# The first layer of a mixture of experts by seven block products on 512 tokens

## The chip, the cores and the metric

The program runs on one core of one Trainium2 chip. The metric is the device time of one execution in microseconds (us), lower is better. The core's engines are PE (TensorE, matrix products), DVE (VectorE), ACT (ScalarE), POOL (GpSimd) and SP (SyncE, which here only issues DMAs). Each works through its own list of instructions in order and waits on semaphores for the others.

## The reference

Attention over q, k, v (2 batches, 8 heads, 576 positions, width 64) gives x of 1152 tokens by 512. Then come two mixtures of experts:

```
p = domain_probs / (domain_probs.sum(-1, keepdims=True) + 1e-09)      # first mixture, 4 experts, all used
for e in range(4):
    h = np.maximum(x @ w1[e], 0.0)                                    # 512 -> 1024
    out += p[:, e:e + 1] * (h @ w2[e])                                # 1024 -> 512
logits = out @ w_gate + modality_bias[modality_id]                    # second mixture, 8 experts
e_idx = argmax(logits)                                                # each token uses one expert
```

The change is in the first mixture, in `x @ w1[e]`.

## The kernel before

Three parts follow one another. The attention and the first steps of the first mixture are ordered by a planner with costs and due times (`Plan`, written out by `emit`). The rest of the first mixture is written by hand as a list of steps. A planned end does the gate and the second mixture.

**Precision.** A float32 product is made of three passes of a rounded format: a tensor is split into a high and a low part (`xhi`, `xlo`; `w1h`, `w1l`; `hh`, `hl`), and high by high, high by low and low by high are added up in PSUM. To split a weight tile, ACT makes the high part (`w_hi`) and DVE the low part (`w_lo`), each over 128x1024 numbers.

**Steps.** The tokens are cut in chunks 0 to 3 of 256, 256, 256 and 384 tokens. `SEG` lists runs of (expert, chunks). A step is (s, c, f): entry s of `SEG`, chunk c, and one of 8 blocks f of 128 hidden units. `mm1` (L693 by the profile) makes `x @ w1` for it in 12 matmuls of 256 columns (4 slices of the width by 3 passes). ACT makes `hh` by a ReLU (L699) and DVE makes `hl` (L704). `mm2` (L712 to L714) multiplies by `w2` in 3 matmuls of 512 columns for each 128 tokens and adds up over f. At f = 7 DVE adds p times the result to `y` (L722, `y_add`). The code writes `mm1` of a step and then `mm2` of the step before, so that PE has work while `hh` and `hl` are made. A scheduler of the compiler then orders each engine's list by what is ready when. Weights come in as 512-KB loads (`raw`, SP) and are split one or two steps ahead.

**Gate work between the steps.** `gate_consts` (called at step (2, 1, 1) before) loads the gate's weights four times in a form spread over all partitions (`st`, L834). POOL copies six of eight experts' columns of each into `wgT` (L835), and later the other two into `wgU` (L859). It also makes a small table `wg` on DVE (L828) and turns the tokens' modality ids into `mf` (DVE, L841), which PE transposes (L843, `ps<-ident,mf`) and DVE combines into `bias`. `dot` (L871, on DVE) multiplies a 128x512 block of finished `y` by one expert's whole row of `wgT` or `wgU` and sums; so the first `dot` needs all four copies. `FIRST` says at which entry of `SEG` a chunk is first summed.

**Memory.** The tiles `st` and the small gate tiles live in the pools `m2raw` and `gate`, which are opened after the attention's pools are closed and take over their memory.

Of the kernel before, what the change touches and what calls it, by code (L numbers as in the profile page):

```python
# [8 lines left out]
F32 = mybir.dt.float32  # L9
F32R = mybir.dt.float32r  # L10
# [7 lines left out]
D = 64  # L18
# [69 lines left out]
TARGET = 3600  # L88
HARD = 3400
TRC = 1  # L90
RUNS = 0
TRR = .75
DP = (50, 20, 0)
DQ = (0, 0, 0, 0, 0, 0)
DMC = 1.23
# [195 lines left out]
def moe_chain_kernel(ctx, tc, q, k, v, probs, w1, w2, mod, wg, mbias, v1, v2, out):  # L291
# [17 lines left out]
    def bank():  # L309
        return ps.tile([128, 512], F32, tag="ps", name="ps")  # L310
# [90 lines left out]
    def tr(nm, n, f):  # L401
        T["pt", nm, n, f] = pt = bank()
        pv = pt[:, 0:RR * RP].rearrange("c (p r) -> c r p", r=RR)
        for r in range(RR):
            x = T[nm, n][:, f]
            if n < RUNS:
                nc.tensor.transpose(pv[0:64, r, :], x[:, D * r:D * r + D], ident[:RP, :RP])
                nc.tensor.matmul(pv[64:128, r, :], x[:, D * (RR + r):D * (RR + r) + D], ident[:RP, :RP], start=True, stop=True)
            else:
                nc.tensor.transpose(pv[:, r, :], x[:, 128 * r:128 * r + 128], ident[:RP, :RP])  # L410
# [245 lines left out]
    W = {}  # L656
    NU = 4

    def w_load(kind, s, j):
        t = rawp.tile([128, KD, 256] if kind == 1 else [128, 2, DM], F32, tag="raw", name="raw")  # L660
        e = SEG[s][0]
        if kind == 1:
# [24 lines left out]
    ACC = {}  # L687

    def mm1_part(o, s, c, f, kk):
        hi, lo = W[1, s, f // 2]  # L690
        fs = slice(128 * (f % 2), 128 * (f % 2) + 128)
# [14 lines left out]
    def mm2_part(s, c, f, t):  # L706
        if f == 0:
            ACC.setdefault((s, c), {})[t] = bank()
        hi, lo = W[2, s, f // 2]
        hh, hl = HT[s, c, f]  # L710
        ts, a = slice(128 * t, 128 * t + 128), ACC[s, c][t]
        nc.tensor.matmul(a, hh[:, ts], hi[:, f % 2, :], start=(f == 0), stop=False)  # L712
        nc.tensor.matmul(a, hh[:, ts], lo[:, f % 2, :], start=False, stop=False)  # L713
        nc.tensor.matmul(a, hl[:, ts], hi[:, f % 2, :], start=False, stop=(f == NF - 1))  # L714
# [834 lines left out]
    if True:  # L1549
# [22 lines left out]
        P.slow, P.lag, P.also = 1.0, 0.0, {}  # L1572
        runs = [(g, c) for g, (_, cs) in enumerate(SEG) for c in cs]
        steps = [z + (f,) for z in runs[:runs.index(QFROM)] for f in range(NF)]
        KP = len([x for x in steps if x[0] < NPSEG]) + 1
        for g in range(NPSEG + 1):
            for j in range(NU):
                for kind in (1, 2):
                    p_w(kind, g, j, (WPR + WST * j if g == 0 else WPG + .1 * (NU * g + j)) + .5 * (kind - 1), WLO)
        for i, z in enumerate(steps[:KP]):  # L1580
            p_mm1(*z, MPR + 1.2 * i)
            if i:
                p_mm2(*steps[i - 1], MPR + 1.2 * i + .5)
        def fillers():
# [11 lines left out]
        m2p["raw"] = ctx.enter_context(tc.tile_pool(name="m2raw", bufs=1, side="right", reuse_waits="tile"))
        m2p["g"] = ctx.enter_context(tc.tile_pool(name="gate", bufs=2, side="right", reuse_waits="tile"))
        y1 = m2p["g"].tile([128, 5, DM], F32, tag="y1", name="y1", bufs=1)
        yacc.extend(y1[:, t, :] for t in range(5))
        dots = [(i, x) for i in range(4) for x in range(V)]  # L1600
        for s, c, f in steps[KP:]:
            mm1(s, c, f)
            mm2(*prev)
            prev = (s, c, f)
            r = runs.index((s, c))
            if c == SEG[s][1][0] and s > NPSEG and f < 2:
# [60 lines left out]
```

## Time and profile before

| | us |
|---|---|
| three runs, median | 625.64 (624.74 to 628.19) |
| the profiled execution | 624.6 |
| its span in the trace | 622.7 |
| PE busy in it | 600.4 (96%) |
| DVE / ACT / POOL busy | 381.8 / 255.2 / 86.9 |
| mean granted PE clock | 0.992 of full |

The span is the time from the first to the last instruction; 1.9 us of the execution lie around it. Busy shares are means over stages. Matmul records overlap (each is shown for longer than the distance to the next), so the pace is read from starts.

### The profile page before, as it was taken

The page shows a single profiled execution, that of the slowest core. Times are in us where ns is not written, and L with a number is a line of the kernel's source. Part 1 is how long each engine was busy: PE and PEld are TensorE (multiplying, and loading weights), DVE is VectorE, ACT ScalarE, POOL GpSimd, SP SyncE. Part 2 cuts the span into 40 slices and gives each one's busy share as a digit, 9 for nine tenths or more (in the row PEclk, how much of TensorE's full clock was granted, in tenths as well). Part 3 has the DMA queues.
Part 4 walks back from the last instruction along what each step waited for, and adds up shares of the span by engine and source line. Part 5 has one row for each costly group of instructions (what it writes and reads, how often), then busy time and mean ns, then how long its engine had stood idle before and what let it go on. Part 6 is the DMA issues. An engine that isn't in the chain of part 4 may idle for free. (4 is left out here: it accounts for less than half of the span.)

```text
span 622.7 us, 11280 instructions
## 1 busy us (share of the span) xinstructions
PE 600.4 (96%) x4265; PEld 527.5 (85%) x4270; DVE 381.8 (61%) x817; ACT 255.2 (41%) x595; POOL 86.9 (14%) x120
## 2 busy tenths in 40 slices
PE   7689999999999999999999999999999999999994
PEld 4578888889798999999989989999988898888983
DVE  4898678767525618564342455439955789669781
ACT  5855256542313411113321334313343555559581
POOL 3333113115000001000000000001130035201011
PEclk9999999999999999999999999999999999999997
DMA  7999944107511510001330345605295404867830
GB/s 148 156 219 221 234 135 136 36 2 213 168 35 61 177 34 2 1 1 52 119 101 1 102 135 173 200 5 132 42 352 193 143 15 131 286 194 254 293 136 20
DMA packets 84465, 78.67 MB, mean 126 GB/s; under 512 B 36135, under 2 KB 67248, under 8 KB 84402
## 3 DMA queue, kind: packets, MB, share of 16 engines
q1 hardware_dynamic: 82482, 73.13, 42.0%
q0 software_dynamic: 1920, 4.73, 2.2%
q8 instruction: 35, 0.57, 0.4%
q14 instruction: 28, 0.23, 0.1%
HBM read 77.49 MB, written 5.07 MB: 133 GB/s over the span
## 5 line engine op out<-in xcount | busy, mean ns | idle before, releaser
L693 PE MATMUL ps<-xhi,w1h 128*128 128x256 f32 (+1 forms) x512 | 153.8, 300 | 0.0
L693 PE MATMUL ps<-xhi,w1l 128*128 128x256 f32 (+1 forms) x512 | 151.8, 297 | 0.0
L693 PE MATMUL ps<-xlo,w1h 128*128 128x256 f32 (+1 forms) x512 | 151.6, 296 | 0.2 <-DVE xlo L609 0.2
L699 ACT ACTIVATE hh<-ps 128x256 fp32r<-128x256 f32 (+1 forms) x128 | 52.4, 410 | 209.6 <-PE ps L693 201.2
L704 DVE SCALAR_TENSOR_TENSOR hl<-ps,hh 128x256 fp32r<-128x256 f32 (+1 forms) x128 | 57.9, 454 | 121.2 <-ACT hh L699 121.0
L712 PE MATMUL ps<-w2h,hh 128*128 128x512 f32 x288 | 115.7, 402 | 0.0
L714 PE MATMUL ps<-w2h,hl 128*128 128x512 f32 x288 | 113.6, 395 | 1.2 <-DVE hl L704 1.2
L713 PE MATMUL ps<-w2l,hh 128*128 128x512 f32 x288 | 113.3, 393 | 0.0
L693 PEld LDWEIGHTS ps<-xhi,w1h 128*128 128x128 f32 x512 | 96.5, 188 | 5.9 <-issue 0.6
L693 PEld LDWEIGHTS ps<-xlo,w1h 128*128 128x128 f32 x512 | 96.4, 188 | 5.3 <-DVE xlo L609 0.4
L693 PEld LDWEIGHTS ps<-xhi,w1l 128*128 128x128 f32 x512 | 96.4, 188 | 0.0
L714 PEld LDWEIGHTS ps<-w2h,hl 128*128 128x128 f32 x288 | 54.0, 188 | 14.8 <-DVE hl L704 2.3
L712 PEld LDWEIGHTS ps<-w2h,hh 128*128 128x128 f32 x288 | 54.2, 188 | 8.0 <-issue 0.4
L713 PEld LDWEIGHTS ps<-w2l,hh 128*128 128x128 f32 x288 | 54.2, 188 | 6.9
L673 DVE TENSOR_TENSOR w2l<-raw,w2h 128x1024 fp32r<-128x1024 f32 x32 | 39.4, 1230 | 29.3 <-ACT w2h L414 29.2
L414 ACT ACTIVATE w1h<-raw 128x1024 fp32r<-128x1024 f32 x47 | 49.7, 1057 | 17.6 <-PE ps L693 14.9
L673 DVE TENSOR_TENSOR w1l<-raw,w1h 128x1024 fp32r<-128x1024 f32 x32 | 39.1, 1221 | 10.8 <-ACT w1h L414 10.1
L414 ACT ACTIVATE w2h<-raw 128x1024 fp32r<-128x1024 f32 x28 | 29.7, 1061 | 37.6 <-PE ps L714 35.6
L1222 DVE TENSOR_TENSOR w2l<-r,w2h 128x1024 fp32r<-128x1024 f32 x28 | 33.9, 1221 | 14.5 <-ACT w2h L414 14.5
L985 POOL DMA_INDIRECT tab<-tg,si x9 | 9.6, 1062 | 209.8 <-DVE tg L982 188.3
L414 ACT ACTIVATE w2h<-r 128x1024 fp32r<-128x1024 f32 x28 | 29.4, 1058 | 17.0 <-PE ps L1345 9.2
L1321 PE MATMUL ps<-xh,w1h 128*128 128x256 f32 x128 | 36.0, 281 | 0.0
(287 smaller groups left out, 933.1 us busy)
## 6 DMA issues: line engine op xcount, KB each, us to landing
raw<-in_moe_w_dram SPq DMA_DIRECT2D x85, 512.0 KB
r<-in_moe_w_dram SPq DMA_DIRECT2D x35, 512.0 KB
v<-in_v_dram SPq DMA_DIRECT2D x32, 80.0 KB
kraw<-in_k_dram SPq DMA_DIRECT2D x16, 147.0 KB
qraw<-in_q_dram SPq DMA_DIRECT2D x16, 147.0 KB
vq<-in_v_dram SPq DMA_DIRECT2D x8, 288.0 KB
ys<-y SPq DMA_DIRECT2D x9, 256.0 KB
st<-in_moe_w_gate_dram SPq DMA_DIRECT2D x4, 512.0 KB
```

The source lines that it names most:

```text
L414: e.activation(out=out, in_=in_, func=ACTF.Copy, scale=scale)
L673: e.tensor_tensor(out=l, in0=W.pop(("raw", kind, s, j)), in1=h.bitcast(F32), op=ALU.subtract)
L693: nc.tensor.matmul(o, wt[:, kk, fs], xt[:, kk, :], start=(kk == 0 and m == 0), stop=(kk == KD - 1 and m == 2))
L699: nc.scalar.activation(out=hh, in_=o, func=ACTF.Relu)
L704: nc.vector.scalar_tensor_tensor(out=hl, in0=o, scalar=0.0, in1=hh.bitcast(F32), op0=ALU.max, op1=ALU.subtract)
L712: nc.tensor.matmul(a, hh[:, ts], hi[:, f % 2, :], start=(f == 0), stop=False)
L713: nc.tensor.matmul(a, hh[:, ts], lo[:, f % 2, :], start=False, stop=False)
L714: nc.tensor.matmul(a, hl[:, ts], hi[:, f % 2, :], start=False, stop=(f == NF - 1))
L985: i = nc.gpsimd.indirect_dma_start(out=tab, out_offset=bass.IndirectOffsetOnAxis(ap=Z["si"][:, t:t + 1], axis=0), in_=G["tg"][:, 3 * c + t ...
L1222: e.tensor_tensor(out=l, in0=R["raw", u], in1=h.bitcast(F32), op=ALU.subtract)
L1321: nc.tensor.matmul(pt, wt[:, kk, fs], xt[:, kk, :], start=(i == 0), stop=(i == 3 * KD - 1))
```

## The change

**What it does.** Entry 3 of `SEG`, expert 3 on all four chunks, becomes two entries, expert 3 on chunks 0 and 1 and expert 3 on chunks 2 and 3; its weights are loaded and split twice. Then `PAIR = (2, 3)`: experts 2 and 3 on the tokens 0 to 511 (chunks 0 and 1 side by side). For expert 2 the hidden blocks (0, 4) and (1, 5) are still done by ordinary steps. The other two pairs of expert 2 and all four of expert 3 are six units. A unit takes two hidden blocks and both chunks, splits the width in halves, and computes the 2x2 product of blocks by Strassen's seven products: `s_mm1` has 7 products of 2 slices by 3 passes, 42 matmuls of 256 columns, where four steps have 48. `s_mm2` has the same 24 matmuls of 512 columns as four `mm2`.

**What feeds a unit.** `s_xf` and `s_xc` make five sums and differences of blocks of x once, split in high and low. `s_w` makes for each unit five sums of weight blocks (`sa`, `sb`) and splits seven blocks. `w_load` brings the w1 columns of a pair as two DMAs of 128 columns. Within a unit the products M4 and M3 go to one bank, `r34`, and ACT copies it (`s34`); M1 goes to a second bank, `r16`, and ACT copies that half (`uv`); M2 and M5 are then added on top of `r34` and M6 and M7 on `r16`. DVE forms the four combinations. The order of the code is `s_mm1` of a unit, then `s_mm2` of the unit before. The expert's second layer is as before.

**What moves.** `gate_consts` is now called at step (4, 2, 1), the second step after the units, `gate_cols` at (4, 2, 4), and the `dot`s start after it. The pools `m2raw` and `gate` are opened only after the pool `seven` of the units is closed, and take over its memory.

```diff
-SEG = ((0, (0, 1)), (1, (0, 1)), (2, (0, 1)), (3, (0, 1, 2, 3)), (2, (2, 3)), (1, (2,)), (0, (2, 3)), (1, (3,)))
+SEG = ((0, (0, 1)), (1, (0, 1)), (2, (0, 1)), (3, (0, 1)), (3, (2, 3)), (2, (2, 3)), (1, (2,)), (0, (2, 3)), (1, (3,)))
+PAIR = (2, 3)
-FIRST = {0: 0, 1: 0, 2: 3, 3: 3}
+FIRST = {0: 0, 1: 0, 2: 4, 3: 4}
...
+    def unit(s, f):
+        return (f % NU, f // NU) if s in PAIR else (f // 2, f % 2)
...
+        if s in PAIR:
+            if kind == 1:
+                for h in range(2):
+                    nc.sync.dma_start(out=t[:, :, 128 * h:128 * h + 128],
+                                      in_=w1[e, :, FF // 2 * h + 128 * j:FF // 2 * h + 128 * j + 128].rearrange("(k p) f -> p k f", p=128))
...
+    def s_w(s, j):
...
+        tt(out=a[:, 0:2].rearrange("p s (k f) -> p (s k) f", k=2), in0=raw[:, :, 1], in1=raw[:, :, 0], op=ALU.subtract)
...
+        nc.scalar.activation(out=ah, in_=a, func=ACTF.Copy)
...
+        tt(out=al, in0=a, in1=ah.bitcast(F32), op=ALU.subtract)
...
+    def s_mm1(s, j):
...
+        def prod(o, i, start):
+            h, l, n, (xh, xl) = m[i]
+            for k in range(2):
+                f = slice(128 * k, 128 * k + 128)
+                for q, (w, x) in enumerate(((h, xh), (h, xl), (l, xh))):
+                    nc.tensor.matmul(o, w[:, n, f], x[:, k], start=start and k == 0 and q == 0, stop=k == 1 and q == 2, skip_group_check=not start)
...
+        r34, r16 = bank(), bank()
+        A, B = slice(0, 256), slice(256, 512)
+        prod(r34[:, B], 4, True)
+        prod(r34[:, A], 3, False)
+        s34, uv, c = t("s34"), t("uv"), t("sc")
+        nc.scalar.activation(out=s34, in_=r34, func=ACTF.Copy)
+        prod(r16[:, A], 1, True)
+        nc.scalar.activation(out=uv[:, B], in_=r16[:, A], func=ACTF.Copy)
+        nc.vector.tensor_tensor(out=uv[:, A], in0=s34[:, A], in1=s34[:, B], op=ALU.add)
+        nc.vector.tensor_tensor(out=uv[:, B], in0=uv[:, A], in1=uv[:, B], op=ALU.add)
+        prod(r16[:, B], 6, False)
+        prod(r34[:, B], 2, False)
+        prod(r34[:, A], 5, False)
+        (h1, l1), (h2, l2) = SH[s, j] = [[t(f"s{x}{i}", F32R) for x in "hl"] for i in range(2)]
+        nc.scalar.activation(out=h2, in_=r34, func=ACTF.Relu)
+        nc.vector.scalar_tensor_tensor(out=l2, in0=r34, scalar=0.0, in1=h2.bitcast(F32), op0=ALU.max, op1=ALU.subtract)
+        prod(r16[:, A], 7, False)
...
+        units = [(2, 2), (2, 3)] + [(3, j) for j in range(NU)]
...
+        for i, (x, j) in enumerate(units):
+            s_mm1(x, j)
+            if i == 0:
+                mm2(*prev)
+            else:
+                s_mm2(*units[i - 1])
...
+            if prev[0] in PAIR:
+                s_mm2(*units[-1])
+                ctxs.close()
+                m2p["raw"] = ctx.enter_context(tc.tile_pool(name="m2raw", bufs=1, side="right", reuse_waits="tile"))
+                m2p["g"] = ctx.enter_context(tc.tile_pool(name="gate", bufs=2, side="right", reuse_waits="tile"))
...
-            if (s, c, f) == (NPSEG, 1, 1):
+            if (s, c, f) == (FIRST[2], 2, 1):
                 gate_consts()
-            if (s, c, f) == (FIRST[2], 2, 1):
+            if (s, c, f) == (FIRST[2], 2, 4):
                 gate_cols()
-            if s >= FIRST[2] and c >= 2 and (s, c, f) > (FIRST[2], 2, 1) and dots:
+            if (s, c, f) > (FIRST[2], 2, 4) and dots:
                 dot(*dots.pop(0))
```

**PE around the transposition of `mf`.** Before, it stands between two steps of expert 3 and waits for nothing; L714 is the third pass of `mm2`, L693 is `mm1`.

```order
L714 MATMUL ps<-w2h,hl 128x512 [waits DVE_49]
L712 MATMUL ps<-w2h,hh 128x512
L713 MATMUL ps<-w2l,hh 128x512
L714 MATMUL ps<-w2h,hl 128x512
L843 MATMUL ps<-ident,mf 128x9
L693 MATMUL ps<-xhi_92,w1h 128x256
L693 MATMUL ps<-xlo_96,w1h 128x256
```

After, the same instruction (L954) stands behind `mm2` of (4, 2, 1), in front of the next `mm1` (L695).

```order
L721 MATMUL ps<-w2h,hl 128x512 [waits DVE_49]
L719 MATMUL ps<-w2h,hh 128x512
L720 MATMUL ps<-w2l,hh 128x512
L721 MATMUL ps<-w2h,hl 128x512
L954 MATMUL ps<-ident,mf 128x9 [waits DVE_49]
L695 MATMUL ps<-xhi_93,w1h 128x256
L695 MATMUL ps<-xlo_97,w1h 128x256
```

It now carries a wait for DVE, and two steps of expert 3 on chunk 2 lie between it and the end of the units.

**DVE around the cast of `mf`.** Before (L841), it stands among splits of weights (L673) and `hl`.

```order
L828 CAST wg<-wr 128x4x8 [waits DMAHW4_49,DMAHW0_49]
L829 TENSOR_TENSOR wg<-wr,wg 128x4x8 [waits DVE_49]
L673 TENSOR_TENSOR w2l<-raw,w2h 128x1024 [waits DMAHW2_49,Activation_49]
L704 SCALAR_TENSOR_TENSOR hl<-ps,hh 128x256 [waits Activation_49]
L673 TENSOR_TENSOR w1l<-raw,w1h 128x1024 [waits DMAHW3_49,PE_49,Activation_49]
L841 CAST mf<-mi 9x128 [waits DMAHW3_49]
```

After (L952), it stands behind three `dot`s (L982), the first of which waits for POOL; five more `dot`s and five small operations lie between it and the next `hl` (L706).

```order
L706 SCALAR_TENSOR_TENSOR hl<-ps,hh 128x256 [waits Activation_49]
L939 CAST wg<-wr 128x4x8 [waits DMAHW7_49]
L940 TENSOR_TENSOR wg<-wr,wg 128x4x8 [waits DVE_49]
L982 SCALAR_TENSOR_TENSOR junk,l<-y_99,wgT 128x512 [waits Pool_49]
L982 SCALAR_TENSOR_TENSOR junk,l<-y_99,wgT 128x512 [waits DVE_49] x2
L952 CAST mf<-mi 9x128 [waits DMAHW3_49]
L982 SCALAR_TENSOR_TENSOR junk,l<-y_99,wgT 128x512 [waits DVE_49]
L957 COPY m<-ps 128x9 [waits PE_49]
```

**SP and the loads of `st` after the change.** Three of the four (L945) carry a wait for PE; POOL copies `wgT` and `wgU` of the first, then of the second, and so on.

```order
L945 DMA st_3459<-in_moe_w_gate_dram 128x1024 [waits PE_49]
L935 DMA tab<-ti 128x164 [waits Pool_49]
L945 DMA st_3462<-in_moe_w_gate_dram 128x1024 [waits PE_49]
L945 DMA st_3465<-in_moe_w_gate_dram 128x1024 [waits PE_49]
L937 DMA wr<-in_moe_w_gate_dram 128x4x8 [waits DMAHW4_49]
L945 DMA st_3468<-in_moe_w_gate_dram 128x1024 [waits DMAHW0_49]
```

They stood at step (2, 1, 1) before, and now stand where the last unit's tiles come free.

**ACT at the end of the planned part.** Before, a `w2h` that waits for PE stands ahead of two `hh` (L699) in a row.

```order
L699 ACTIVATE hh<-ps 128x256 [waits DVE_49,PE_49]
L414 ACTIVATE w1h<-raw 128x1024 [waits DMAHW3_49]
L414 ACTIVATE w2h<-raw 128x1024 [waits DMAHW1_49,PE_49]
L699 ACTIVATE hh<-ps 128x256 [waits DVE_49]
L699 ACTIVATE hh<-ps 128x256 [waits DVE_49,PE_49]
L414 ACTIVATE w2h<-raw 128x1024 [waits DMAHW6_49,PE_49]
```

After, the copies of `s_xc` (L771, `sx`) stand there too.

```order
L701 ACTIVATE hh<-ps 128x256 [waits PE_49,Activation_49]
L404 ACTIVATE w1h<-raw 128x1024 [waits DMAHW5_49,DMAHW4_49]
L771 ACTIVATE sx_2473<-sc 128x512 [waits DVE_49]
L701 ACTIVATE hh<-ps 128x256 [waits PE_49,Activation_49]
L404 ACTIVATE w2h<-raw 128x1024 [waits DMAHW6_49,PE_49]
L771 ACTIVATE sx_2473<-sc 128x512 [waits DVE_49]
L701 ACTIVATE hh<-ps 128x256 [waits PE_49,Activation_49]
```

The `hh` of a step now stands ahead of the next `w2h`, one `hh` between two splits.

## Rows read from the trace of the kernel before

**Rows 1.** The page's busy times: us, share of the span, instructions.

```profile
PE 600.4 (96%) x4265; PEld 527.5 (85%) x4270; DVE 381.8 (61%) x817; ACT 255.2 (41%) x595; POOL 86.9 (14%) x120
```

**Rows 2.** Timeline of PE in undisturbed steps: start, us, engine, line, operation.

```profile
200.11 0.28 PE L693 MATMUL ps<-xhi,w1h 128*128 128x256 f32 x1
...
201.42 0.28 PE L693 MATMUL ps<-xhi,w1l 128*128 128x256 f32 x1
201.54 0.40 PE L712 MATMUL ps<-w2h,hh 128*128 128x512 f32 x1
...
202.93 0.28 PE L693 MATMUL ps<-xhi,w1h 128*128 128x256 f32 x1
```

**Rows 3.** Timeline of PE around a stall.

```profile
155.01 0.28 PE L693 MATMUL ps<-xhi,w1h 128*128 128x256 f32 x1
...
157.91 0.50 PE L714 MATMUL ps<-w2h,hl 128*128 128x512 f32 x1 [0.58 <-DVE hl L704]
158.25 0.39 PE L712 MATMUL ps<-w2h,hh 128*128 128x512 f32 x1
...
158.95 0.28 PE L693 MATMUL ps<-xhi,w1h 128*128 128x256 f32 x1
```

**Rows 4.** Timeline of ACT at that stall.

```profile
155.20 1.06 ACT L414 ACTIVATE w2h<-raw 128x1024 fp32r<-128x1024 f32 x1 [2.88 <-PE ps L714]
156.17 0.86 ACT L699 ACTIVATE hh<-ps 128x256 fp32r<-128x256 f32 x2
```

**Rows 5.** Timeline of ACT, one `hh` of an undisturbed step.

```profile
201.74 0.39 ACT L699 ACTIVATE hh<-ps 128x256 fp32r<-128x256 f32 x1 [1.62 <-PE ps L693]
```

**Rows 6.** Groups of ACT by line and shape: busy, mean ns | idle before.

```profile
L912 ACT ACTIVATE yT<-ps 128x512 fp32r<-128x512 f32 x3 | 1.6, 599 | 0.0
```

**Rows 7.** Timeline of SP's DMA queue, the loads of `st`.

```profile
139.62 0.35 SPq L834 DMA_DIRECT2D st<-in_moe_w_gate_dram  x1
...
140.55 0.89 SPq L834 DMA_DIRECT2D st<-in_moe_w_gate_dram  x2
```

**Rows 8.** Timeline of POOL, the copies into `wgT` and `wgU`.

```profile
143.66 1.75 POOL L835 COPY wgT<-st 128x768 f32<-128x768 f32 x1 [16.02 <-DMA st<-in_moe_w_gate_dram]
146.51 4.16 POOL L835 COPY wgT<-st 128x768 f32<-128x768 f32 x2 [1.10 <-DMA st<-in_moe_w_gate_dram]
152.57 2.58 POOL L835 COPY wgT<-st 128x768 f32<-128x768 f32 x1 [1.89 <-DMA st<-in_moe_w_gate_dram]
232.83 2.55 POOL L859 COPY wgU<-st 128x256 f32<-128x256 f32 x4 [77.68 <-PE ps L693]
```

**Rows 9.** Timeline of DVE around the gate's small tables.

```profile
148.99 1.72 DVE L828 CAST wg<-wr 128x32 fp32r<-128x32 f32 x1
150.75 0.19 DVE L829 TENSOR_TENSOR wg<-wr,wg 128x32 fp32r<-128x32 f32 x1
150.85 1.22 DVE L673 TENSOR_TENSOR w2l<-raw,w2h 128x1024 fp32r<-128x1024 f32 x1
...
153.50 1.73 DVE L841 CAST mf<-mi 9x128 f32<-9x128 int32 x1
```

**Rows 10.** Timeline of DVE, `dot`s, `hl` and `y`.

```profile
239.06 0.42 DVE L704 SCALAR_TENSOR_TENSOR hl<-ps,hh 128x256 fp32r<-128x256 f32 x1
239.39 0.69 DVE L871 SCALAR_TENSOR_TENSOR junk<-y,wgT 128x512 f32<-128x512 f32 x1
...
240.12 0.69 DVE L871 SCALAR_TENSOR_TENSOR junk<-y,wgT 128x512 f32<-128x512 f32 x1
...
258.98 1.40 DVE L722 SCALAR_TENSOR_TENSOR y<-ps,p,y 128x512 f32<-128x512 f32 x2
```

**Rows 11.** Stretches of PE in the attention: busy, granted clock, DMA share, GB/s.

```profile
29.30:30.00 0.70, 0.12 (x1) 0.50 0.48 100
...
32.00:33.00 1.00, 1.00 (x5) 0.67 1.05 198
```

**Rows 12.** Timeline of PE there.

```profile
29.88 0.61 PE L492 MATMUL ps<-ident,da 128*72 128x128 f32 x2 [2.43 <-DVE da L487]
```

More of the change, by code (lines that the diff above doesn't have):

```diff
@@ L90 @@
 TRC = 1
-RUNS = 0
-TRR = .75
 DP = (50, 20, 0)
@@ L404, in tr @@
         for r in range(RR):
[L405 to L410, printed above, removed]
+            nc.tensor.transpose(pv[:, r, :], T[nm, n][:, f, 128 * r:128 * r + 128], ident[:RP, :RP])
     def copy(e, out, in_, scale=1.0):
@@ L661, in w_load @@
         e = SEG[s][0]
-        if kind == 1:
+        if s in PAIR:
[4 more added lines that the diff above has]
+            else:
+                nc.sync.dma_start(out=t, in_=w2[e].rearrange("(h j p) f -> j p h f", h=2, p=128)[j])
+        elif kind == 1:
             nc.sync.dma_start(out=t, in_=w1[e, :, 256 * j:256 * j + 256].rearrange("(k p) f -> p k f", p=128))
@@ L689, in mm1_part @@
     def mm1_part(o, s, c, f, kk):
-        hi, lo = W[1, s, f // 2]
-        fs = slice(128 * (f % 2), 128 * (f % 2) + 128)
+        j, g = unit(s, f)
+        hi, lo = W[1, s, j]
+        fs = slice(128 * g, 128 * g + 128)
         for m, (wt, xt) in enumerate(((hi, xhi[c]), (hi, xlo[c]), (lo, xhi[c]))):
@@ L708, in mm2_part, with mm2_rows @@
             ACC.setdefault((s, c), {})[t] = bank()
-        hi, lo = W[2, s, f // 2]
         hh, hl = HT[s, c, f]
[L711 to L714, printed above, removed]
+        ts = slice(128 * t, 128 * t + 128)
+        mm2_rows(s, c, f, t, hh[:, ts], hl[:, ts])
+    def mm2_rows(s, c, f, t, hh, hl):
+        j, g = unit(s, f)
+        hi, lo = W[2, s, j]
+        a = ACC[s, c][t]
+        nc.tensor.matmul(a, hh, hi[:, g, :], start=(f == 0), stop=False)
+        nc.tensor.matmul(a, hh, lo[:, g, :], start=False, stop=False)
+        nc.tensor.matmul(a, hl, hi[:, g, :], start=False, stop=(f == NF - 1))
     def y_add(s, c, t):
@@ L735, in mm2, with s_open, s_xf @@
                 y_add(s, c, t)
+    ST = {}
+    SH = {}
+    def s_open():
+        ctxs = ExitStack()
+        ST["p"] = ctxs.enter_context(tc.tile_pool(name="seven", bufs=2, side="right", reuse_waits="tile"))
+        ST["x"] = [ST["p"].tile([128, 5, 2, 256], F32R, tag=f"sx{i}", name=f"sx{i}", bufs=1) for i in range(2)]
+        ST["f"] = [ST["p"].tile([128, KD, 256], F32, tag=f"sf{i}", name=f"sf{i}", bufs=1) for i in range(2)]
+        return ctxs
+    def s_xf(c):
+        nc.vector.tensor_tensor(out=ST["f"][c], in0=xhi[c].bitcast(F32), in1=xlo[c].bitcast(F32), op=ALU.add)
@@ new lines, in s_xc @@
+    def s_xc(i):
+        b11, b21, b12, b22 = [ST["f"][c][:, k:k + 2, :] for c in range(2) for k in (0, 2)]
+        hi, lo = [x[:, i] for x in ST["x"]]
+        a, b, op = ((b11, b22, ALU.add), (b12, b22, ALU.subtract), (b21, b11, ALU.subtract), (b11, b12, ALU.add), (b21, b22, None))[i]
+        o = ST["p"].tile([128, 2, 256], F32, tag="sc", name="sc")
+        if op is None:
+            nc.vector.scalar_tensor_tensor(out=o, in0=a, scalar=-1.0, in1=b, op0=ALU.mult, op1=ALU.subtract)
+        else:
+            nc.vector.tensor_tensor(out=o, in0=a, in1=b, op=op)
+        nc.scalar.activation(out=hi, in_=o, func=ACTF.Copy)
+        nc.vector.tensor_tensor(out=lo, in0=o, in1=hi.bitcast(F32), op=ALU.subtract)
@@ L737, in p_w, with s_mm2 @@
+    def s_mm2(s, j):
+        h = SH.pop((s, j))
+        for t in range(4):
+            c = t // 2
+            if s == 3 and j == 0:
+                ACC.setdefault((s, c), {})[t % 2] = bank()
+            for g in range(2):
+                hh, hl = [x[:, 256 * g + 128 * (t % 2):256 * g + 128 * (t % 2) + 128] for x in h[c != g]]
+                mm2_rows(s, c, j + NU * g, t % 2, hh, hl)
+            if j == NU - 1:
+                y_add(s, c, t % 2)
     def p_w(kind, s, j, pr, off):
@@ L1574, in moe_chain_kernel @@
         steps = [z + (f,) for z in runs[:runs.index(QFROM)] for f in range(NF)]
+        late = [z for z in steps if z[0] > PAIR[-1]]
         KP = len([x for x in steps if x[0] < NPSEG]) + 1
@@ L1577, in moe_chain_kernel @@
             for j in range(NU):
-                for kind in (1, 2):
+                for kind in (1, 2) if g < NPSEG or j < 2 else (2,):
                     p_w(kind, g, j, (WPR + WST * j if g == 0 else WPG + .1 * (NU * g + j)) + .5 * (kind - 1), WLO)
@@ L1583, in moe_chain_kernel @@
                 p_mm2(*steps[i - 1], MPR + 1.2 * i + .5)
+        P.op("PE", 0.0, lambda: None, r=[("wh", 2, NPSEG, j) for j in range(NU)], prio=1e6)
         def fillers():
@@ L1595, in moe_chain_kernel @@
         ctxa.close()
[L1596 to L1599, printed above, removed]
+        ctxs = s_open()
+        w_load(1, 2, 2)
+        for i, z in enumerate((c, f) for j in (0, 1) for c in range(2) for f in (j, j + NU)):
+            if i:
+                mm1(2, *z)
+                mm2(*prev)
+                prev = (2,) + z
+            if i < 2:
+                s_xf(i)
+            elif i < 7:
+                s_xc(i - 2)
+            if i == 4:
+                w_load(1, 2, 3)
+            if i == 5:
+                s_w(2, 2)
+                w_load(1, 3, 0)
@@ new lines, in moe_chain_kernel @@
+        units = [(2, 2), (2, 3)] + [(3, j) for j in range(NU)]
+        s_w(2, 3)
+        w_load(2, 3, 0)
+        for i, (x, j) in enumerate(units):
+            s_mm1(x, j)
+            if i == 0:
+                mm2(*prev)
+            else:
+                s_mm2(*units[i - 1])
+            if i + 2 < len(units):
+                s_w(*units[i + 2])
+                w_load(*((1,) + units[i + 3] if i + 3 < len(units) else (1, 4, 0)))
+            else:
+                w_split(1, 4, i - 4)
+                w_load(1, 4, i - 3)
+            if i < 4:
+                w_split(2, 3, i)
+                w_load(2, *((3, i + 1) if i < 3 else (4, 0)))
+            else:
+                w_split(2, 4, i - 4)
+                w_load(2, 4, i - 3)
@@ L1600, in moe_chain_kernel @@
+        y1 = None
         dots = [(i, x) for i in range(4) for x in range(V)]
-        for s, c, f in steps[KP:]:
+        for s, c, f in late:
             mm1(s, c, f)
-            mm2(*prev)
+            if prev[0] in PAIR:
[3 more added lines that the diff above has]
+                m2p["g"] = ctx.enter_context(tc.tile_pool(name="gate", bufs=2, side="right", reuse_waits="tile"))
+                y1 = m2p["g"].tile([128, 5, DM], F32, tag="y1", name="y1", bufs=1)
+                yacc.extend(y1[:, t, :] for t in range(5))
+            else:
+                mm2(*prev)
@@ L1604, in moe_chain_kernel @@
             prev = (s, c, f)
+            if (s, c) == late[0][:2] and f < 4:
+                w_split(1 + f % 2, s, 2 + f // 2)
+                if f < 2:
+                    w_load(1 + f, s, 3)
             r = runs.index((s, c))
-            if c == SEG[s][1][0] and s > NPSEG and f < 2:
+            if c == SEG[s][1][0] and s > late[0][0] and f < 2:
                 w_split(1 + f, s, 3)
```

37 lines of the change are left out of this document (30 added, 7 removed).

## The prediction, made before the changed kernel had run

> **What bounds the kernel now.** I read the page's busy times first: PE is busy 600.4 of 622.7 us [rows 1], so PE sets the end and every removed matmul counts at its full pace, as long as nothing makes PE wait. The timeline of PE in undisturbed steps gives that pace: eleven distances between matmuls of 256 columns take 201.42 - 200.11 = 1.31, or 0.119 each; six of 512 columns take 202.93 - 201.54 = 1.39, or 0.232 each; a step takes 2.82 [rows 2]. Then I looked for PE's waits in the stretch that is changed. There are two of one kind: the step that starts at 155.01 takes 3.94 instead of 2.82 because its `hl` comes late [rows 3], and ACT shows why: `w2h` waited 2.88 us for PE and stood ahead of two `hh` [rows 4]. The second one, a few steps on, is alike, 1.1 us too. Last I followed what `gate_consts` needs, since it is moved: loads of `st` [rows 7], copies on POOL [rows 8], small operations on DVE [rows 9] and the dots [rows 10].
>
> **The change part by part.** All of it is set against the profiled execution's 624.6 us (span 622.7 and 1.9 around it); the median of the runs, 625.6, lies 1.0 above that.
>
> *Matmuls saved.* Six units have 42 instead of 48 matmuls of 256 columns: 36 × 0.119 = **-4.3**. `s_mm2` has the same 24 of 512 as before. A unit is then 42 × 0.119 + 24 × 0.232 = 10.6 us of PE.
>
> *The two stalls.* In the new order of ACT, `hh` stands ahead of the next `w2h` and only one lies between two splits. I take both stalls as gone: 2 × 1.1 is 2.2, less 0.3 for copies `sx` of half such a length that now stand there: **-1.9**, between -2.2 and 0 (they stay).
>
> *A wait within the unit.* M2 is added onto the bank `r34`, so PE must wait until ACT has copied it to `s34`. ACT starts 0.32 after the start of the last matmul (201.42 to 201.74) [rows 2, 5], a copy of 512 columns takes 0.60 [rows 6], a semaphore back some 0.05 (a choice of mine): 0.97. Seven matmuls after that last start are hidden behind M1: 7 × 0.119 = 0.83. So 0.14 is open, and a matmul after a wait is followed at 0.34 (157.91 to 158.25) instead of 0.23 [rows 3]: 0.25 a unit, six units, **+1.5**. Nothing in the trace shows the unit itself, so the bounds are 0.8 (only the open part) and 2.5 (the copy of M1's half behind a split of 1.06 on ACT [rows 4] in some units).
>
> *New work on DVE and ACT.* In a unit DVE has splits and sums at 1.22 for 1024 columns [rows 9], 0.7 for 512 and 0.42 for 256 [rows 10]: 9.1 us by my count of the unit's instructions, against 10.6 of PE. I cost it at nothing; the cover is that 10.6, and it is thin. Two units also carry four `y` additions of 0.7 [rows 10] and reach 12: if PE has to wait for these, +3. ACT has about 5.4 a unit and the loads of twice the weights of expert 3 have ten microseconds each: nothing.
>
> *The moved gate constants.* This is the largest term. Let E be the end of the last unit's `s_mm2`. Before, nothing waited at the transposition of `mf`. Now PE meets it after one more `mm1` and two `mm2`: 1.42 + 2 × 1.39 [rows 2], E + 4.2. What has `mf` to go through? The tiles `st` take over the memory of the units, so loads wait for PE's last products there; I take that as E. Landing: 139.62 to 143.66 is 4.04, and 140.55 to 146.51 is 5.96 [rows 7, 8]; I take 5.0 and 0.1 for the issue, E + 5.1. POOL then still has three copies `wgT` and two `wgU`. Alone a `wgT` took 1.75, beside DVE up to 2.58, and `wgU` 2.55 / 4 = 0.64 [rows 8]; DVE waits here, so 3 × 1.75 + 2 × 0.64 = 6.5, E + 11.6. The first `dot` reads all four copies; on DVE, in order, three `dot`s stand ahead of the cast of `mf`. A `dot` takes 0.73 (239.39 to 240.12) [rows 10]: E + 13.8. The cast then takes 0.2, by the small operation at 150.75 [rows 9] that had no POOL beside it, not the 1.73 of the cast at 153.50 [rows 9]; E + 14.0. PE stands from E + 4.2: **+9.8**. Bounds: landing 4.04 gives 8.8; landing 5.96, copies at 2.58 and the cast at 1.73 give 14.8. Behind the waiting transposition all of PE's list is queued, so all of it is paid.
>
> The cast of `wg` at 148.99 took 1.72 and ended where POOL's pair of copies ended, and so did the cast of `mf` at 153.50 with the next copy [rows 8, 9]. The Trainium skill (SBUF — State Buffer, "SBUF: two separate sides") says that DVE and GpSimd share one pair of ports, which one instruction holds to its end while the other waits. The trace agrees with it. By that rule the first `dot` would also wait for the last `wgU` (0.64), and the sum would be 0.6 higher.
>
> *After the wait.* In the attention PE waited 2.43 us until 29.88 [rows 12]; the granted clock was then 0.50 at 29.3 to 30, and 0.67 as a mean of 32 to 33, which is half for two thirds of it and full for the rest [rows 11]. PE thus worked 2.8 us at half pace and lost 1.4. I expect the same here; twice that is the upper bound, none the lower. At the same time DVE has five `dot`s, five small operations and a split `hl` before PE can go on: 5 × 0.73 + 5 × 0.1 + 0.33 = 4.5 [rows 9, 10], where PE wants it 2 × 1.42 + 0.46 = 3.3 after its start [rows 2]. The next six intervals hold 2, 3, 4, 4, 3 and 5 `dot`s; against 2.82 a step the lag on DVE is at its largest 1.9 (after the last). Clock and lag lie under each other, not in a row: **+1.9**, between 0 and 4.7.
>
> Sum: 624.6 - 4.3 - 1.9 + 1.5 + 9.8 + 1.9 = 631.6 for an execution like the profiled one; plus 1.0, **632.6** for the median.
>
> **The rivals.** *A, the gate is not late (other side, faster).* If the `st` loads come free 9.8 us earlier than I hold, because they wait for something that PE does well before E, or if DVE reaches the cast of `mf` before the first `dot`, the transposition finds `mf` ready. The point is E + 4.2: ready by then, both last terms go and 624.6 - 4.3 - 1.9 + 1.5 = 619.9 is left, 620.9 for the median. For it: before, the same chain cost nothing. Against it: in the order of the built kernel the loads carry waits for PE, and the cast stands behind `dot`s that wait for POOL. 0.07.
>
> *B, half the wait.* If the loads wait only for the last unit's products and not for its `s_mm2` (24 × 0.232 = 5.6 earlier), the wait is 4.2, the loss after it about 1.5, and the sum 625.6, 626.6 for the median. 0.08.
>
> *C, units bound by DVE.* If the 9.1 us of DVE come late to PE in the two units with `y` additions (+3), or small losses in all six add up to that much, the time is 635.6, to 638 with the wait's upper half. For it: the thin cover; against it: DVE's work on weights can be done a unit ahead. 0.2.
>
> *D, the saving isn't there.* The number of matmuls is in the built code; that they are slower than 0.119 nothing in the trace suggests, since the units use the same shape. 0.02, with 637.
>
> **How the numbers follow.** My forecast as summed has 0.63, C 0.2, B 0.08, A 0.07, D 0.02. The likeliest is 632.6. The range goes from 627.5, the upper side of B and below the sum of all lower bounds (624.6 - 4.3 - 2.2 + 0.8 + 8.8 + 0 + 1.0 = 628.7), to 640, which holds C and the wait's upper bound (+5) but not all upper bounds at once. Left out are A and most of B and a few hundredths above. Half a per cent, about what a measurement of this kernel can tell from no change, is 622.5 to 628.8 here: faster 0.07 (A), the same 0.08 (B), slower 0.85.
>
> **What would show it right or wrong.** In the new profile: PE has 36 matmuls fewer, and units of 10.6 to 10.9 us in its timeline; a single wait of about 10 us at `ps<-ident,mf`, released by DVE; POOL idle before `wgT` of the second `st` with a DMA as releaser, some 5 us after E; three `dot`s directly behind the last `wgT`; a granted clock of about 0.5 just behind the wait; no idle time of 0.58 at `hl` in the planned part; within units an idle of 0.1 to 0.3 before M2, released by ACT. The forecast is wrong if the wait at the transposition is under 5 us, or if idle time of PE inside the units, released by DVE, sums to over 3.

## The result and the profile after

| | before | after |
|---|---|---|
| median of six runs, us | 626.42 (624.74 to 628.19) | 633.38 (632.16 to 637.08) |
| ratio after / before | | 1.0104, 95% interval 1.0069 to 1.0138 |
| span of the profiled execution | 622.7 | 635.1 |
| mean granted PE clock | 0.992 | 0.977 |

The changed kernel is slower by about 1%, 7.0 us by the medians, where 632.6 was forecast. The first part of the page of the changed kernel (busy us, share of the span, instructions) answers to [rows 1]:

```profile
PE 602.2 (95%) x4229; PEld 527.7 (83%) x4234; DVE 423.3 (67%) x883; ACT 277.3 (44%) x628; POOL 83.9 (13%) x120
```

PE has the 36 matmuls fewer (4229 for 4265) and is busy 602.2 of 635.1 us: what it gained in count, it lost in waiting and in clock.

The timeline of PE of the changed kernel (start, us, engine, line, operation, idle time before and its releaser) at the end of the units and behind it:

```profile
254.32 0.28 PE L695 MATMUL ps<-xhi,w1h 128*128 128x256 f32 x1
...
258.52 0.50 PE L721 MATMUL ps<-w2h,hl 128*128 128x512 f32 x1 [0.74 <-DVE hl L706]
...
267.47 0.27 PE L954 MATMUL ps<-ident,mf 9*128 9x9 f32 x1 [7.75 <-DVE mf L952]
267.67 0.58 PE L695 MATMUL ps<-xhi,w1h 128*128 128x256 f32 x1
...
272.32 0.39 PE L719 MATMUL ps<-w2h,hh 128*128 128x512 f32 x1
...
273.72 0.28 PE L695 MATMUL ps<-xhi,w1h 128*128 128x256 f32 x1
```

PE ends the units at 254.32 (E). It should meet the transposition 4.2 later, at 258.5. It issues it at 267.47, 9.0 late: it waited 0.74 for `hl` and 7.75 for the cast of `mf`. The two `mm1` behind it take 272.32 - 267.67 = 4.65 instead of 2.84. The stretches of PE (start and end, length, busy and instructions, granted clock, DMA share, GB/s), which answer to [rows 11], show that the clock stays low there:

```profile
270.00:271.00 1.00, 1.00 (x6) 0.50 0.00 0
...
272.00:274.00 2.00, 2.00 (x14) 1.00 0.00 0
```

What releases the transposition is read backwards, on DVE, POOL and SP (timelines of the changed kernel, one fence for each engine):

```profile
255.61 2.52 DVE L674 TENSOR_TENSOR w2l<-raw,w2h 128x1024 fp32r<-128x1024 f32 x1 [0.34 <-ACT w2h L404]
...
261.18 1.47 DVE L940 TENSOR_TENSOR wg<-wr,wg 128x32 fp32r<-128x32 f32 x1
264.71 1.09 DVE L982 SCALAR_TENSOR_TENSOR junk<-y,wgT 128x512 f32<-128x512 f32 x1 [2.06 <-POOL wgT L946]
...
267.20 0.21 DVE L952 CAST mf<-mi 9x128 f32<-9x128 int32 x1
...
271.18 0.42 DVE L706 SCALAR_TENSOR_TENSOR hl<-ps,hh 128x256 fp32r<-128x256 f32 x1
```

```profile
258.89 1.64 POOL L946 COPY wgT<-st 128x768 f32<-128x768 f32 x1 [0.26 <-DMA st<-in_moe_w_gate_dram]
...
261.05 1.55 POOL L946 COPY wgT<-st 128x768 f32<-128x768 f32 x1
...
263.12 1.55 POOL L946 COPY wgT<-st 128x768 f32<-128x768 f32 x1
264.62 0.64 POOL L970 COPY wgU<-st 128x256 f32<-128x256 f32 x1
```

```profile
254.28 0.81 SPq L945 DMA_DIRECT2D st<-in_moe_w_gate_dram  x2
...
262.68 0.31 SPq L948 DMA_DIRECT2D mi<-in_moe_modality_id_dram  x1
```

and the sum of waits of SP's queue from 245 to 263 (us in total, times, longest):

```profile
SPq L945 <- PE ps L721: 3.3, 1, 3.3
```

The second and third `st` are issued at 254.28, released by PE's last `mm2`, at E as supposed. The first of them has landed when POOL begins to copy at 258.89; the last `wgT` ends at 264.67; the first `dot` could start then; three `dot`s later the cast of `mf` runs, in 0.21, and PE goes on. A second chain runs beside it: `mi` is loaded only at 262.68, since it takes over the tile of `wr`, which the operation at 261.18 still reads. When that load had landed no row shows; the cast at 267.20 did not wait for it.

One more line of the profiled execution answers to nothing before. In the planned end PE waits 5.11 us for a weight split:

```profile
527.52 0.79 PE L1455 MATMUL ps<-w2l,dh 128*128 128x512 f32 x1 [5.11 <-DVE w2l L1333]
```

and its clock behind that is low (the stretch of PE, columns as above):

```profile
527.50:531.00 3.50, 3.48 (x8) 0.51 0.41 95
```

The wait is 5.1 of the 12.4 by which the two spans differ, and some 1.8 more go at half clock behind it (3.5 us of work at half pace). A kernel without the units has such a wait too (below); without it the two profiled executions differ by 5.5.

### The profile page after: what moved, and what is told of

Read it like the earlier page. It is cut to its first block, busy times and chain, and to the rows that moved or that the text cites. A ratio compares the mean times of both kernels' runs of the same rounds, so it can differ in the third digit from the quotient of the medians.

```text
span 635.1 us, 11351 instructions
## 1 busy us (share of the span) xinstructions
PE 602.2 (95%) x4229; PEld 527.7 (83%) x4234; DVE 423.3 (67%) x883; ACT 277.3 (44%) x628; POOL 83.9 (13%) x120
## 4 chain that ended last, share of the span: by engine, by line
PE 85%; DVE 4%; issue 4%; DMA 2%; ACT 1%; POOL 1%; another core or an unknown queue 1%; SPq 1%; POOLq 0%; ACTq 0%
PE ps L695 27%; PE ps L719 11%; PE ps L721 10%; PE ps L720 10%; PE ps L1432 7%; PE ps L809 5%; PE ps L1455 2%; PE ps L1454 2%; PE ps L1456 2%; PE ps L585 1%; DMA kraw<-in_k_dram 1%; PE ps L400 1%; DMA st<-in_moe_w_gate_dram 1%; PE ps L456 1%
## 5 line engine op out<-in xcount | busy, mean ns | idle before, releaser
L695 PE MATMUL ps<-xhi,w1h 128*128 128x256 f32 (+1 forms) x416 | 128.0, 308 | 0.0
L695 PE MATMUL ps<-xlo,w1h 128*128 128x256 f32 (+1 forms) x416 | 125.7, 302 | 0.3 <-DVE xlo L599 0.3
L695 PE MATMUL ps<-xhi,w1l 128*128 128x256 f32 (+1 forms) x416 | 125.6, 302 | 0.0
L719 PE MATMUL ps<-w2h,hh 128*128 128x512 f32 x240 | 96.6, 403 | 0.0
L706 DVE SCALAR_TENSOR_TENSOR hl<-ps,hh 128x256 fp32r<-128x256 f32 (+1 forms) x104 | 47.8, 461 | 72.0 <-ACT hh L701 71.6
L721 PE MATMUL ps<-w2h,hl 128*128 128x512 f32 x240 | 94.8, 395 | 0.7 <-DVE hl L706 0.7
L720 PE MATMUL ps<-w2l,hh 128*128 128x512 f32 x240 | 94.4, 393 | 0.0
L695 PEld LDWEIGHTS ps<-xhi,w1h 128*128 128x128 f32 x416 | 79.7, 191 | 4.8 <-issue 0.6
L695 PEld LDWEIGHTS ps<-xlo,w1h 128*128 128x128 f32 x416 | 79.6, 191 | 4.4 <-DVE xlo L599 0.5
L695 PEld LDWEIGHTS ps<-xhi,w1l 128*128 128x128 f32 x416 | 79.5, 191 | 0.0
L721 PEld LDWEIGHTS ps<-w2h,hl 128*128 128x128 f32 x240 | 45.1, 188 | 11.9 <-DVE hl L706 1.2
L1432 PE MATMUL ps<-xl,w1h 128*128 128x256 f32 x128 | 35.8, 280 | 0.0
```

The costliest lines, as they stand in the source:

```text
L706: nc.vector.scalar_tensor_tensor(out=hl, in0=o, scalar=0.0, in1=hh.bitcast(F32), op0=ALU.max, op1=ALU.subtract)
L719: nc.tensor.matmul(a, hh, hi[:, g, :], start=(f == 0), stop=False)
L720: nc.tensor.matmul(a, hh, lo[:, g, :], start=False, stop=False)
L721: nc.tensor.matmul(a, hl, hi[:, g, :], start=False, stop=(f == NF - 1))
L1432: nc.tensor.matmul(pt, wt[:, kk, fs], xt[:, kk, :], start=(i == 0), stop=(i == 3 * KD - 1))
```

## Experiments

Ratios are to the kernel before, in runs on the same chip.

**The modality part called later.** The load of `mi`, the cast, the transposition and `bias` become a function of their own, called at step (4, 3, 1).

```diff
+    def gate_bias():
+        g = m2p["g"]
...
+            if (s, c, f) == (FIRST[2],) + (3, 1):
+                gate_bias()
```

> Only the modality part of the gate's constants (load of mi, cast mf, its transposition on PE, and bias) is called two chunks of steps later, at step (4, 3, 1). In the built order the transposition then stands in front of the steps on chunk 3, and two more hl stand ahead of the first dot on DVE, so that the next hl after the dots is the one of (4, 2, 4). Theory (the loss is PE standing at the transposition while DVE stands at the dots): no wait at the transposition, no half clock after it; 633.4 - 9.3 - 1.8 - 0.7 (the stall at 258.5) = 621.6, faster than the kernel before by about 4.7. Rival (the units of seven products don't gain, or lose on DVE): still 626 or more. Second rival (the wait only moves to the next hl behind the dots): 630 to 633.

Measured: 622.18 (619.74 to 628.48, 12 runs), ratio 0.9918 (0.9884 to 0.9953): faster than both kernels, 11.2 below the changed one by the medians, and 9.2 below its second measurement (last experiment). DVE of this kernel around the first `dot`:

```profile
260.35 0.42 DVE L706 SCALAR_TENSOR_TENSOR hl<-ps,hh 128x256 fp32r<-128x256 f32 x1 [0.74 <-ACT hh L701]
263.17 0.42 DVE L706 SCALAR_TENSOR_TENSOR hl<-ps,hh 128x256 fp32r<-128x256 f32 x1 [2.39 <-ACT hh L701]
...
266.47 1.17 DVE L990 SCALAR_TENSOR_TENSOR junk<-y,wgT 128x512 f32<-128x512 f32 x1 [1.64 <-POOL wgT L946]
...
267.57 0.41 DVE L706 SCALAR_TENSOR_TENSOR hl<-ps,hh 128x256 fp32r<-128x256 f32 x1
```

and PE there, with no idle time at all, and at the transposition, now far behind:

```profile
255.47 0.28 PE L695 MATMUL ps<-xhi,w1h 128*128 128x256 f32 x1
...
262.55 0.40 PE L719 MATMUL ps<-w2h,hh 128*128 128x512 f32 x1
...
283.03 0.22 PE L962 MATMUL ps<-ident,mf 9*128 9x9 f32 x1
```

DVE still stands 1.64 us at the first `dot` until the last `wgT`. But two more `hl` lie ahead of it (260.35, 263.17), and the one behind it (267.57) is ready when PE wants it. From E (255.47) to the `mm2` of (4, 2, 2) at 262.55 it takes 7.1 us, in the changed kernel 254.32 to 272.32, 18.0: 10.9 less, about what the time fell by. The units gain, and the wait didn't move to the next `hl`; both rivals fall. The edit changes two orders at once, the place of the transposition on PE and, by the scheduler, that of the `hl`s and the `dot`s on DVE; the next experiment leaves the transposition where it was and moves only the cast.

**`wr` with memory of its own.** `mi` no longer shares a tile with `wr`, and the scheduler puts the cast of `mf` ahead of the `dot`s, with the transposition in its old place.

```diff
-        wr = g.tile([128, 256], F32, tag="tmp", name="wr", bufs=1)[:, 0:KD * V].rearrange("p (k e) -> p k e", k=KD)
+        wr = g.tile([128, KD * V], F32, tag="wr", name="wr", bufs=1).rearrange("p (k e) -> p k e", k=KD)
```

> One change against the changed kernel: wr has a tile of its own, so mi is loaded without waiting for wg. In the built order the cast of mf then stands ahead of the dots on DVE, the transposition in its old place on PE. If being behind the dots were all, PE would stand only until about 260 and the time would fall by some 7.5 to 9, to 624.5 to 626. Theory: DVE still stands at the first dot until the last wgT (264.7), and five dots and small operations stand ahead of the next hl; PE then waits for that hl from about 263 to 269, so the loss is mostly paid again: about 3.5 saved, 630.

Measured: 633.28 (627.76 to 635.88, 10 runs), ratio 1.0078 (1.0044 to 1.0112), not distinct from the changed kernel. Its PE, its DVE, SP and POOL (one fence each):

```profile
256.66 0.28 PE L695 MATMUL ps<-xhi,w1h 128*128 128x256 f32 x1
...
264.70 0.27 PE L954 MATMUL ps<-ident,mf 9*128 9x9 f32 x1 [3.65 <-DVE mf L952]
...
273.07 0.50 PE L721 MATMUL ps<-w2h,hl 128*128 128x512 f32 x1 [3.27 <-DVE hl L706]
...
274.10 0.28 PE L695 MATMUL ps<-xhi,w1h 128*128 128x256 f32 x1
```

```profile
263.95 0.69 DVE L952 CAST mf<-mi 9x128 f32<-9x128 int32 x1 [2.53 <-DMA mi<-in_moe_modality_id_dram]
268.34 1.14 DVE L982 SCALAR_TENSOR_TENSOR junk<-y,wgT 128x512 f32<-128x512 f32 x1 [3.69 <-POOL wgT L946]
...
272.60 0.42 DVE L706 SCALAR_TENSOR_TENSOR hl<-ps,hh 128x256 fp32r<-128x256 f32 x1
```

```profile
258.61 0.31 SPq L948 DMA_DIRECT2D mi<-in_moe_modality_id_dram  x1
```

```profile
262.44 1.55 POOL L946 COPY wgT<-st 128x768 f32<-128x768 f32 x1 [1.07 <-DMA st<-in_moe_w_gate_dram]
```

The transposition waits 3.65 instead of 7.75, and 3.27 come back at the next `hl`, which is made at 272.60 behind five `dot`s. From E (256.66) to the `mm1` at 274.10 it takes 17.4; the changed kernel takes 254.32 to 273.72, 19.4 for the same work. So 2.0 were saved there of 3.5 expected, and the medians don't show it. What the expectation missed lies on POOL: it has the second `st` only at 262.44, 5.8 behind E, where the changed kernel has it 4.6 behind E (258.89). So the first `dot` starts 11.7 behind E instead of 10.4 (268.34 and 264.71), and with it the `hl` behind the `dot`s, for which PE then waits. The load of `mi` came late too: it was issued at 258.61, and the cast began at 263.95 after 2.53 us of waiting for it. But had it come earlier, PE would only have stood longer at that `hl`, which waits for the `dot`s and not for `mi`. What follows is that the transposition's place behind the `dot`s is only a part of the matter: DVE itself stands at the first `dot`, and whatever PE needs from behind it comes late.

**The late place without the units.** In the kernel before, the three calls are moved as the change moves them.

```diff
-            if (s, c, f) == (NPSEG, 1, 1):
+            if (s, c, f) == (FIRST[2], 2, 1):
                 gate_consts()
-            if (s, c, f) == (FIRST[2], 2, 1):
+            if (s, c, f) == (FIRST[2], 2, 4):
                 gate_cols()
-            if s >= FIRST[2] and c >= 2 and (s, c, f) > (FIRST[2], 2, 1) and dots:
+            if s >= FIRST[2] and c >= 2 and (s, c, f) > (FIRST[2], 2, 4) and dots:
```

> The kernel before with the three gate calls moved to the later steps as in the change (gate_consts at (3, 2, 1), gate_cols at (3, 2, 4), dots after), but without units, so the memory of the gate tiles is free early. Theory (the memory that comes free late is what delays the loads, not the place in the code): the loads and the cast still run early, no wait at the transposition, 626.4, the same as before within 0.3%. Rival (the place in the code costs it): 632 or more.

Measured: 629.33 (624.29 to 631.89, 10 runs), ratio 1.0008 (0.9975 to 1.0040): the same as before, though the median of the ten lies 2 above, a spread that the last experiment comes back to. SP, DVE and PE of this kernel:

```profile
138.86 0.35 SPq L834 DMA_DIRECT2D st<-in_moe_w_gate_dram  x1
```

```profile
154.25 1.62 DVE L841 CAST mf<-mi 9x128 f32<-9x128 int32 x1 [0.89 <-DMA mi<-in_moe_modality_id_dram]
```

```profile
261.47 0.22 PE L843 MATMUL ps<-ident,mf 9*128 9x9 f32 x1
```

The scheduler issues the first load at 138.86, as before [rows 7], and casts `mf` at 154.25, a hundred microseconds ahead of the transposition at 261.47, which waits for nothing. The place in the code costs nothing where the memory is free: the late loads of the changed kernel come from the memory that the units hold until E. The direct counterpart, memory of their own for the tiles `st` beside the units, was not tried.

**Expert 3 in two entries, nothing else.**

```diff
-... (3, (0, 1, 2, 3)), ...
+... (3, (0, 1)), (3, (2, 3)), ...
-FIRST = {0: 0, 1: 0, 2: 3, 3: 3}
+FIRST = {0: 0, 1: 0, 2: 4, 3: 4}
```

> The kernel before with expert 3 cut in two entries, its weights loaded and split twice, nothing else. Theory: loads and splits are hidden, the same within 0.3% (626.4). Rival (eight more loads of 512 KB and eight more splits cost): 2 to 5 us more.

Measured: 625.91 (624.90 to 631.85, 10 runs), ratio 0.9995 (0.9957 to 1.0033). The second load of the weights is hidden. PE still has the two stalls in the planned part, as [rows 3]:

```profile
158.22 0.51 PE L714 MATMUL ps<-w2h,hl 128*128 128x512 f32 x1 [0.58 <-DVE hl L704]
```

The second is at 164.98, with 0.59. Neither stands in any profile of a kernel with units.

**One product twice.** On top of the first experiment, the six matmuls of M4 are issued twice, the second time over the first.

```diff
         prod(r34[:, B], 4, True)
+        prod(r34[:, B], 4, True)
```

> Against the kernel with the late modality part (622.2): in each unit the six matmuls of the first product (M4) are issued twice, the second time over the first, so a unit has 48 matmuls again, the number of four ordinary steps. Theory (PE is the bound in the units, each matmul counts at full pace): 36 x 0.119 = 4.3 more, 626.5, the part of a unit in its first layer 5.32 + 0.71 = 6.03. Rival (the units wait for DVE or ACT and the saved matmuls are partly idle time anyway): less than 2 more.

Measured: 625.80 (623.43 to 631.66, 12 runs), ratio 0.9992 (0.9955 to 1.0029); 3.6 above the first experiment by the medians, 4.6 by the two ratios. A unit's first layer in its timeline of PE:

```profile
204.12 0.40 PE L809 MATMUL ps<-sx,w1h 128*128 128x256 f32 x2
...
210.16 0.40 PE L719 MATMUL ps<-w2h,sh 128*128 128x512 f32 x1
```

takes 210.16 - 204.12 = 6.04, as worked out (6.03). The saved matmuls count at full pace, and with them put back the kernel has about the time of before.

**The second layer inside the unit.** On top of the first experiment, `mm2` of the unit before is written behind M1.

```diff
-    def s_mm1(s, j):
+    def s_mm1(s, j, mid):
...
+        mid()
         prod(r16[:, B], 6, False)
```

> Against the kernel with the late modality part (622.2): the second layer of the unit before is written inside the unit, behind M1, so that PE has work while ACT copies r34. If the 0.32 by which a unit's first layer (5.32) is longer than 42 x 0.119 = 5.0 is this wait, up to 6 x 0.32 = 1.9 less, 620.3. Rival: the low parts of the unit before come too late for the earlier place (they have 2.1 us instead of 5.3), PE waits there for DVE: 1 to 2 us a unit, 628 to 634.

Measured: 620.71 (618.42 to 624.38, 4 runs), ratio 0.9872 (0.9802 to 0.9943), not told apart from the first experiment by its interval. Nor does the trace show a gain: from the first unit's start to the `mm1` of (4, 2, 3) it takes 261.23 - 187.30 = 73.93, in the first experiment 261.11 - 187.20 = 73.91. A wait of PE for ACT is still there, 0.31 at 218.23 in the fourth unit. The experiment is inconclusive on what the wait within the units could give back.

**The changed kernel again.**

> The changed kernel itself once more, for a second profile on the chip of these runs. Theory: 633 again; the wait at the transposition of about 8 and the half clock behind it again; the wait of 5.1 at 527 in the first profile, where a weight split in the planned end came late, belongs to that execution and not to the kernel: without it the span is about 630.

Measured: 631.42 (630.17 to 639.20, 10 runs), ratio 1.0071 (1.0031 to 1.0111). Its PE:

```profile
268.95 0.27 PE L954 MATMUL ps<-ident,mf 9*128 9x9 f32 x1 [8.16 <-DVE mf L952]
```

```profile
529.34 0.80 PE L1455 MATMUL ps<-w2l,dh 128*128 128x512 f32 x1 [5.45 <-DVE w2l L1333]
```

The wait at the transposition is there again, 8.16. So is the one in the planned end, 5.45, in an execution that took 639.2 while the other nine took 630.2 to 635.5. That it belonged to the first profile alone was wrong. But it isn't the change's: the kernel before with the gate calls moved has it in its profile (PE idle 4.54 before 520.40), at 630.24 us. In the chain of work of the changed kernel that ended last (start, us, what) it begins on ACT:

```profile
519.19 1.05 ACT w2h L404
520.24 5.18 another core or an unknown queue
```

ACT stands 5.2 us behind a `w2h`, for something that the profile can't name, and DVE and PE then wait for ACT. Three of the nine profiles of this study have it, with 5.2, 5.2 and 4.4; three others, the first experiment's and the two built on it, have waits of ACT without a name of 0.8 to 2.3 in the planned end. What it is stays open. It is of the size by which the runs of one kernel spread here (5 to 9 us); that it makes this spread is likely and not shown.

## Why the prediction was right

The forecast was 632.6 and the result 633.38, and each term of the sum that showed has its row; the lag on DVE did not come. Profiled executions are compared by the starts of the same matmul.

- **Up to the end of the units.** Forecast -4.3 - 1.9 + 1.5 = -4.7. The matmul behind the units starts at 259.42 before and at 254.32 after: -5.1. Of it 2.4 lie ahead of the first unit (188.47 before, 186.08 after), where the two stalls are gone (2 x 1.1) and the 0.3 put down for the copies `sx` did not come, and 2.7 in the units, where -4.3 + 1.5 = -2.8 was forecast.
- **The wait within the unit** was put at 0.25 and is 0.29 in these timelines of PE and ACT of the changed kernel:

```profile
216.52 0.27 PE L809 MATMUL ps<-sx,w1l 128*128 128x256 f32 x1
216.83 0.38 PE L809 MATMUL ps<-xhi,w1h 128*128 128x256 f32 x1
217.05 0.28 PE L809 MATMUL ps<-xlo,w1h 128*128 128x256 f32 x1
```

```profile
216.18 0.60 ACT L819 ACTIVATE s<-ps 128x512 f32<-128x512 f32 x1 [0.43 <-PE ps L809]
```

  0.31 and 0.22 stand where 0.12 each would do, and M2 begins at 216.83, 0.05 after ACT ends the copy of `r34` (216.78): the mechanism is the one that was said, and so is the 0.05 that was chosen for the semaphore. The four later units have 0.29 each, the first 0.23, the second, where matmuls of `s_mm2` fall in between, 0.17: 1.6 in all for 1.5.
- **DVE in the units** was costed at nothing, with 9.1 us of work to 10.6 of PE. The stretches of the second and the third unit (start and end, length; PE, PEld, DVE, ACT, POOL busy; clock; DMA share; GB/s) show

```profile
192.76:203.55 10.79, 10.79 (x67) 9.52 (x66) 10.79 (x22) 5.65 (x10) 0.00 (x0) 1.00 0.39 112
203.55:214.48 10.93, 10.90 (x67) 9.59 (x66) 9.12 (x15) 5.25 (x9) 0.00 (x0) 1.00 0.28 84
```

  DVE at 10.79 of 10.79 and at 9.12 of 10.93, ACT at 5.65 and 5.25 (5.4 was said). In the second unit DVE has no idle time at all, so there the cover was gone; in the last two it is busy 6.8 of 10.9. Still PE waits for DVE nowhere in the units. Rival C didn't come.
- **The wait at the transposition** was forecast as 9.8: landing 5.0, copies 6.5, three `dot`s 2.2, cast 0.2, less the 4.2 of work that PE has. The rows give 4.6 from issue (254.28) to the first copy (258.89), 5.8 from there to the end of the last `wgT` (264.67), 2.5 from there to the cast (267.20), and 0.2 for the cast. PE goes on 267.47 - 258.5 = 9.0 late. Each piece of the chain was the right one; the landing was 0.4 shorter than the middle of the two rows that I took, the copies were a little faster than the row of before (1.55 to 1.64 for 1.75), and the `dot`s took 0.3 more.
- **POOL beside DVE.** The first `dot` took 1.09 instead of the usual 0.69 [rows 10], beside the last `wgU` (264.62, 0.64 long), and the small operation at 261.18 took 1.47 where [rows 9] have 0.19, and ended with the copy `wgT` that began at 261.05. The split at 255.61 took 2.52 where [rows 9] have 1.22, beside the first copy `wgT` (255.34 to 257.05); it holds up the `hl` for which PE stands 0.74 at 258.52, a wait that the forecast did not have and that the larger one behind it covers. The trace agrees with the port that DVE and POOL share (the Trainium skill, SBUF — State Buffer, "SBUF: two separate sides"). By that rule 0.6 more was said; 0.4 came, inside the 9.0.
- **After the wait** 1.9 was forecast, as the larger of clock and lag. The two `mm1` lost 4.65 - 2.84 = 1.8 at a granted clock of 0.50, the lower of the two levels. That the two figures agree is luck: the 1.9 was the lag's, and the clock, which did cost 1.8, had been put at 1.4. The lag on DVE cost nothing. The first `hl` behind the `dot`s was ready at 271.6; PE wanted it at 272.8, and at 271.0 had the clock not held it back, so 0.6 of lag lay under the clock. The `hl` after the last of the six intervals, where the lag was to be largest, stands in these timelines of DVE and PE:

```profile
288.36 0.55 DVE L706 SCALAR_TENSOR_TENSOR hl<-ps,hh 128x384 fp32r<-128x384 f32 x1
```

```profile
291.07 0.39 PE L721 MATMUL ps<-w2h,hl 128*128 128x512 f32 x1
```

  It was ready at 288.9, 2.2 before PE wanted it, which is more than the 1.8 by which the clock had put PE back.
- **Together** the gate cost 272.32 - 266.50 + 5.1 = 10.9 us (266.50 is the start of the same `mm2` before), where 11.7 was forecast, and the first experiment gives it back.

Rival B (loads released by the last products, not by the last `mm2`) fell by SP's row: 254.28, released by `ps` of L721. Rival A needed `mf` by E + 4.2; the first experiment, in which PE does not wait there, shows about what it would have given: 622.18, for which 620.9 was worked out.

What the sum couldn't hold is the planned end. The forecast set the change at +7.0 (631.6 against 624.6). The rows give -5.1 + 10.9 = +5.8, the two profiled executions without the 5.1 and its clock +5.5, and the two measurements of the changed kernel +6.5 and +4.4 by their ratios (1.0104 and 1.0071 of 626.4). So the mechanism and the size are right, and the rows lie between the two measurements; that the first median came within 0.8 of the forecast is in part luck, since the terms add up to 1.2 less than was said.

## What to carry to other kernels

A part that takes memory for a while moves everything that is to use that memory afterwards, loads and copies included; when the matmuls saved are few, look first at who is queued behind the late loads on each in-order engine. Two engines can wait for the same late load at once, and then taking it out of one queue gives little (2.0 of 10.9 here), while moving the waiting operation to where its input is old gives all of it back. A wait of TensorE can be paid again behind it, where the clock is low for a while.

## What was not expected of the hardware

In the kernel with `wr` of its own, the load of `mi`, 9 x 256 numbers, took 5.3 us behind three loads of `st`, of which the first, 512 KB, was with POOL 5.8 us after its issue. In the same kernel the clock was 0.50 behind the wait of 3.65 us, and 1.00 behind the one of 3.27 us that ended at 273.07 (stretches of its PE, columns as above):

```profile
264.70:267.00 2.30, 2.30 (x11) 0.50 0.17 61
273.00:276.00 3.00, 2.93 (x18) 1.00 0.00 0
```

Why they differ stays open. ACT's wait in the planned end comes in some executions, with the units (5.2 us, twice) and without them (4.4 us), without a releaser in the profile.
